# Row scores 48 slots ahead, key tiles loaded earlier and in pairs, weight stores one tile later, and output copies tied to TensorE, in an attention and MLP block on one core

## The chip, the core and the metric

The kernel runs on one core of one Trainium2 chip. The metric is the device time of one launch in microseconds (us). A core has five engines that run their own instruction streams in order: PE (TensorE, matrix multiply), DVE (VectorE), ACT (ScalarE), POOL (GpSimd) and SP (SyncE, which here does nothing but issue DMAs). They meet only through semaphores. An instruction that waits holds back all that stands behind it on its engine.

## The reference

One transformer block for 2048 rows of width 576, with 32 heads of 18 and an MLP of width 4608, all in f32:

```python
mod = (silu(c) @ w_mod).reshape(1, 6, 1, 576)
sa, ca, ga, sb, cb, gb = mod[:, 0], ..., mod[:, 5]
h = layernorm(x) * (1 + ca) + sa
q, k, v = heads(h @ wqkv)                      # 32 heads of 18
p = softmax(q @ k.T * 18 ** -0.5)
x = x + ga * ((p @ v) @ wo)
h = layernorm(x) * (1 + cb) + sb
x = x + gb * (silu(h @ w1) @ w2)               # 576 -> 4608 -> 576
```

## The kernel before

**Tiling.** The queries are cut into four blocks of 512 rows (b = 0 to 3), the heads into eight quads of four. A quad of one block is 32 *slots*. In slot s two score products stand on PE, in two half-slots j = 0 and 1:

- `psa` (`slot_mm`): 128 queries against 512 keys of one head, rows of scores. DVE takes their maximum into `mx` (L692). When a quad's 32 slots are through, `max_a` and `max_rows` turn the maxima, write them to DRAM (`mscr<-mt`, L717) and read them back as two extra rows of the query tile (`qt<-mscr`, L721).
- `psb` (`slot_b`): 128 keys against 512 queries, the transposed scores with the maxima already taken off by those two rows. ACT takes the exponential into a tile `pt` (L741).

`psa` runs `LEAD` slots ahead of `psb`, since a quad's `psb` needs the maxima of all its `psa`. The two of one half-slot use opposite halves of the array's rows and run side by side. The values products `psv` (L776, four heads of one 128-key tile at a time) read `pt` and use the whole array; `PB` tiles `pt` are in turn use.

**Key tiles.** `ka0..3` feed `psa`, `kb0..3` feed `psb`. A *chunk* is 512 keys of a quad: two tiles, one for each pair of heads (`hp`). `load_k` issues a chunk's four DMAs in one go, 8 slots before the chunk's first use, at the slot in which the tiles' last use has just been issued.

**Fillers.** Between the score and values products PE gets other work, from a list (`Filler`). For b = 0 it is the rest of the q and k projections (`psqk`), whose weights are loaded by DMAs that ACT issues (`qk_load`, L529). Then, while block b + 1 is in attention, it is block b's output projection, second layernorm and MLP (`post`). Block 3's MLP runs alone at the end. Products are made in f32 accuracy from a high and a low part of each operand. In the first pass over the MLP weights (`first`, beside block 1's attention) `weights` loads each piece raw into one of three buffers, POOL splits it (L836 to L838), and the split tile is stored to DRAM (`w1s`, `w2s`, `wos`, L839); later passes read the split tiles back (L829). The adds into the residual `x` are partly ACT copies `gt` (L899) followed by POOL adds (L900).

**What sets the order.** PE's order is written out by a planner in the kernel: `Plan` keeps a clock of PE and of the queues of ACT ("A") and DVE ("V"), with a fixed cost per operation (`TMAX` for a row maximum, `TEXP` for an exponential), and the loop at the end takes values products, a filler piece or a half-slot, whichever its rules allow. The start (layernorm 1, v and first q, k projections, the first `LEAD` slots' `psa`) is ordered by a small list scheduler (`Start`). On ACT, DVE, POOL and SP the framework orders the instructions by its own estimate of when each is ready.

Of the kernel before, what the change touches and what calls it, by code (L numbers as in the profile page):

```python
# [18 lines left out]
P = 128  # L19
# [6 lines left out]
KT = 5  # L26
# [13 lines left out]
LEAD = 40  # L40
# [3 lines left out]
NKA, NKB = 4, 4  # L44
KLD = 8
# [16 lines left out]
PB = 10  # L62
# [12 lines left out]
TMAX, TEXP = 690, 600  # L75
# [24 lines left out]
class Plan:  # L100
# [22 lines left out]
    def advance(self):  # L123
        while True:
            best = None
            for e, q in self.queue.items():
                if q:
                    s = max(self.free[e], q[0][0])
                    if s <= self.t and (best is None or s < best[0]):
                        best = s, e  # L130
            if best is None:
                return
            s, e = best
            _, _, dur, done = heapq.heappop(self.queue[e])
            self.free[e] = s + dur
            if done is not None:
                done(s + dur)
# [203 lines left out]
def tile_adaln_block(ctx: ExitStack, tc: tile.TileContext, x, wqkv, wo, w1, w2, c, wfirst, wcol, out):  # L341
# [14 lines left out]
    kas = [at1.tile([P, 512], F32R, name=f"ka{i}") for i in range(NKA)]  # L356
    kbs = [at1.tile([P, 512], F32R, name=f"kb{i}") for i in range(NKB)]
# [99 lines left out]

    class Pair:
# [137 lines left out]
    state = {"now": 0, "p": 0, "ka": 0, "kb": 0, "b": 0, "tail": False, "tail2": False}  # L596
# [3 lines left out]
    def add_qk(steps):  # L600
        def load(i):
            which, m, _ = steps[i]
            fill.add(0, lambda: qk_w.update({i: qk_load(which, m, i)}))

        for i, (which, m, pairs) in enumerate(steps):
            for n in sum(pairs, ()):
                names = [("qkx"[which], m, n)]
                for p in range(len(GQ)):
                    fill.add(MMC * len(GQ[p]), lambda i=i, which=which, m=m, n=n, p=p: qk_one(which, m, n, qk_w[i], p), name=names, need=bank_need if p == 0 else None, mode="full")
                    if n == pairs[0][0] and p == 0 and i + 1 < len(steps):  # L610
                        load(i + 1)
                    if i >= MI and p == len(GQ) - 1 and mods:
# [3 lines left out]
                        fill.add(200, lambda a=mt_: mod_piece(*a), mode="full")  # L616

# [37 lines left out]
    def load_k(ring, n):  # L655
        i, kc = divmod(n, NKEY)
        qd = i % NQUAD
        tiles = kas if ring == "a" else kbs
        for hp in range(2):
            kt_ = tiles[state["k" + ring] % len(tiles)]  # L660
            state["k" + ring] += 1
            h = 4 * qd + 2 * hp
            for j in range(2):
                nc.sync.dma_start(f(kt_[64 * j:64 * j + 54, :]),
                                  f(kscr[(h + j) * DH:(h + j + 1) * DH, :, kc * 512:(kc + 1) * 512].rearrange("d c s -> (d c) s")))
            quads.setdefault(i, {})[ring, kc, hp] = kt_
# [10 lines left out]
    def slot_load(s):  # L677
        i = s // 32
        if s % 32 == (22 if i == 0 else 14) and i + 1 < NQ:
# [43 lines left out]
    def slot_b(s, j):  # L723
# [3 lines left out]
        if j == 0:  # L727
            if s % 8 == 0 and s and s + 8 < 32 * NQ:
                load_k("b", s // 8 + 1)
# [5 lines left out]
            t["P"][kt, hp] = pts[s % PB]  # L735
# [3 lines left out]
        mm(ps, lhsT=t["b", kt // 4, hp][64 * e:64 * e + 56, kt % 4 * P:(kt % 4 + 1) * P],  # L739
# [86 lines left out]
    def weights(w, src, scr, first, gate=None):  # L826

        if not first:
            nc.sync.dma_start(f(w), f(scr))  # L829
            return  # L830
        n = w.shape[2] // 2
        for cs in (slice(0, n), slice(n, 2 * n)):
            raw = mp["p"].tile([P, 320], F32, tag="raw", name="raw", bufs=3)[:, :n]
            nc.sync.dma_start(raw, src[:, cs])
            if gate is not None:
                nc.gpsimd.tensor_tensor(raw, raw, gate[:, cs], op=ALU.mult)  # L836
            nc.gpsimd.tensor_copy(w[:, 1, cs], raw)
            nc.gpsimd.tensor_tensor(w[:, 0, cs], raw, f(w[:, 1, cs]), op=ALU.subtract)  # L838
        nc.sync.dma_start(f(scr), f(w))  # L839

# [15 lines left out]
    def post(b):  # L856
# [7 lines left out]
        def o_T(kt):  # L864
# [7 lines left out]
            nc.scalar.activation(hi[:n], src[:n], AF.Copy)  # L872
# [179 lines left out]
        def add_mlp1(i, w2n=()):  # L1052

            for part in range(NG):
# [34 lines left out]
    def start_tasks(st):  # L1089
# [285 lines left out]
        for n in range(2 * NKB):  # L1375
            ones_t.append(dma(40e3, lambda n=n: nc.sync.dma_start(f(kbs[n // 2][64 * (n % 2) + 54:64 * (n % 2) + 56, :]), f(oscr[:, :512])), [t], 8.4))
        q_in = [dma(443e3, lambda: load_quad(0), stored[QM, 0, 0], 5.5)]
        for kc in range(4):
            k_in[0, kc] = dma(443e3, lambda kc=kc: load_k("b" if kc < 2 else "a", kc), stored[KM, 0, kc] + ([k_in[0, kc - 1]] if kc else []), 5.5 + kc)
# [3 lines left out]
        for s in range(LEAD):  # L1383
            i, w = divmod(s, 32)
            if s in (24, 32):
                kc = s // 8 - 3
                k_in[1, kc] = dma(443e3, lambda kc=kc: load_k("a", 4 + kc), stored[KM, 0, kc] + stored[KM, 1, kc] + [mm_t, k_in[(0, 3) if kc == 0 else (1, 0)]], 10 if kc else 8.8)
# [77 lines left out]
    while now < 2 * (total + LEAD) or pend or later:  # L1465
        plan.advance()
        if not mp and fill.pos == len(fill.items):
# [7 lines left out]
        room = state["p"] + (now % 2 == 0) <= PB  # L1475
# [7 lines left out]
        elif not mp:  # L1483
# [98 lines left out]
```

## Time and profile before

| | us |
|---|---|
| median of 3 runs | 2464.89 |
| lowest and highest | 2458.97, 2471.31 |
| profiled execution | 2463.14 |
| its span | 2461.4 |
| PE busy in the span | 2359.8 |
| DVE busy | 1789.9 |
| ACT busy | 1497.0 |
| POOL busy | 628.6 |

How to read it: the span goes from the first to the last instruction of the profiled execution, whose own time is 1.7 us longer. "Busy" is the union of an engine's instructions. The ends of PE's matmuls are modelled, so a short wait can hide inside a busy PE. Times in rows are counted from the span's start. In a row of the timeline the bracket holds the idle time of the engine just before the row and what ended it; "x4" is a row of four instructions. The stages by time: start to 168, attention of block 0 with the q and k fillers to 537, the change to the MLP pools and the first output projection to 600, block 1 with the first pass over the weights to about 1143, block 2 to 1668, block 3 to 2172, then block 3's MLP alone.

### The profile page before, as it was taken

What the parts mean: (1) busy time and instruction counts of PE and PEld (TensorE: products, weight loads), DVE (VectorE), ACT (ScalarE), POOL (GpSimd) and SP (SyncE); (2) the same over time, 40 slices, a digit from 0 to 9 for tenths busy, and PEclk for the clock granted to TensorE, in tenths of its full rate; (3) what the DMA queues carried; (4) which work ended last, traced back from release to release, by engine and by line L of the source; (5) the groups of instructions that cost most, each with busy time, mean ns of one, the idle gap of its engine ahead of it and who ended that gap; (6) DMA issues with size and microseconds to landing.
All of it is one profiled execution on the core that took longest, in us unless ns stands there. A gap on an engine that the chain in (4) does not pass through costs nothing.

```text
span 2461.4 us, 52349 instructions
## 1 busy us (share of the span) xinstructions
PE 2359.8 (96%) x19952; PEld 1585.1 (64%) x19952; DVE 1789.9 (73%) x3110; ACT 1497.0 (61%) x2736; POOL 628.6 (26%) x763
## 2 busy tenths in 40 slices
PE   6989999998999999999999999998999999989999
PEld 4864444433556666766667667775666766678998
DVE  7868888876777888777888888887888788234333
ACT  4227777765566777666677677775677677732121
POOL 5201111122565666554211111112211111110000
PEclk9999999999899999999999999999999999999999
DMA  7744445454466676664545554453655454426563
GB/s 242 250 154 151 147 150 161 143 160 146 144 202 195 227 227 209 206 211 164 182 147 202 171 178 157 164 179 117 217 176 162 155 197 165 133 90 241 183 214 119
DMA packets 201458, 433.01 MB, mean 176 GB/s; under 512 B 31354, under 2 KB 67610, under 8 KB 201210
## 3 DMA queue, kind: packets, MB, share of 16 engines
q1 hardware_dynamic: 196618, 427.37, 52.4%
q8 instruction: 160, 2.62, 0.5%
q10 hardware_dynamic: 4592, 2.29, 0.4%
q14 instruction: 88, 0.72, 0.1%
HBM read 338.53 MB, written 86.33 MB: 173 GB/s over the span
## 4 chain that ended last, share of the span: by engine, by line
PE 82%; DMA 6%; DVE 5%; POOL 2%; ACT 2%; issue 2%; SPq 1%; ACTq 0%; POOLq 0%; DVEq 0%
PE ps L480 25%; PE psv L776 17%; PE psa L690 12%; PE ps L474 10%; PE psb L739 8%; PE psqk L561 4%; DVE mx L692 2%; PE psv L480 2%; PE psp L480 1%; DMA raw<-in_w 1%; DMA mscr<-mt 1%; PE psv L1238 1%; PE psqk L1238 1%; PE psqk L480 1%; PE psp L474 1%
## 5 line engine op out<-in xcount | busy, mean ns | idle before, releaser
L692 DVE TENSOR_REDUCE mx<-psa 128x1 f32<-128x512 f32 x2048 | 1333.0, 684 | 334.5 <-PE psb L739 199.6
L741 ACT ACTIVATE pt<-psb 128x512 f32<-128x512 f32 x2048 | 1150.5, 598 | 511.0 <-PE psb L739 350.0
L739 PE MATMUL psb<-qt,kb 56*128 56x512 f32 x2048 | 772.6, 427 | 39.2 <-ACT pt L741 22.0
L690 PE MATMUL psa<-ka,qt 54*128 54x512 f32 x2016 | 739.4, 420 | 10.9 <-DVE mx L692 8.7
L690 PEld LDWEIGHTS psa<-ka,qt 54*128 54x128 f32 x2016 | 344.1, 188 | 316.3 <-DVE mx L692 213.4
L776 PE MATMUL psv<-pt,vt 128*32 128x512 f32 x4096 | 521.4, 608 | 2.0 <-ACT ov L780 2.0
L480 PE MATMUL ps<-w2t,g 64*128 64x288 f32 x4992 | 418.4, 296 | 0.2
L739 PEld LDWEIGHTS psb<-qt,kb 56*128 56x128 f32 x2048 | 357.4, 187 | 90.3 <-ACT pt L741 61.0
L480 PEld LDWEIGHTS ps<-w2t,g 64*128 64x128 f32 x4992 | 390.7, 188 | 32.7 <-DVE mx L692 13.4
L480 PE MATMUL ps<-hh,w1t 64*128 64x512 f32 x2160 | 384.7, 395 | 1.7 <-DVE x L896 1.6
L480 PEld LDWEIGHTS ps<-hh,w1t 64*128 64x128 f32 x2160 | 216.4, 186 | 60.6 <-DVE mx L692 10.9
L1016 POOL TENSOR_TENSOR g<-etmp,g 128x512 fp32r<-128x512 f32 x108 | 138.8, 1305 | 397.6 <-ACT g L1015 318.0
L776 PEld LDWEIGHTS psv<-pt,vt 128*32 128x32 f32 x4096 | 98.5, 109 | 211.7 <-issue 203.4
L900 POOL TENSOR_TENSOR x<-x,gt 128x288 f32<-128x288 f32 x116 | 92.7, 801 | 427.0 <-ACT gt L899 426.9
L480 PE MATMUL ps<-hl,w1t 64*128 64x512 f32 x864 | 181.1, 392 | 0.0
L896 DVE TENSOR_TENSOR x<-ps,x 128x288 f32<-128x288 f32 x184 | 83.8, 456 | 122.0 <-PE ps L474 76.6
L474 PE MATMUL ps<-w2t,g 128*128 128x288 f32 x960 | 132.9, 299 | 7.4 <-ACT g L1015 5.9
L474 PEld LDWEIGHTS ps<-w2t,g 128*128 128x128 f32 x960 | 130.6, 191 | 9.9 <-ACT g L1015 6.3
L1012 ACT ACTIVATE eq<-ps 128x512 f32<-128x512 f32 x36 | 21.5, 598 | 146.4 <-PE ps L474 146.4
L474 PE MATMUL ps<-hh,w1t 128*128 128x512 f32 x360 | 106.9, 390 | 0.5 <-DVE hh L415 0.5
L480 PEld LDWEIGHTS ps<-hl,w1t 64*128 64x128 f32 x864 | 90.5, 187 | 16.5
L1013 DVE SCALAR_TENSOR_TENSOR etmp<-etmp 128x512 f32<-128x512 f32 x108 | 78.1, 759 | 22.1 <-ACT etmp L1012 21.3
(141 smaller groups left out, 2025.4 us busy)
## 6 DMA issues: line engine op xcount, KB each, us to landing
w1t<-w1s SPq DMA_DIRECT2D x108, 640.0 KB
w2t<-w2s SPq DMA_DIRECT2D x108, 576.0 KB
kb<-kscr SPq DMA_DIRECT2D x512, 108.0 KB
ka<-kscr SPq DMA_DIRECT2D x504, 108.0 KB
w1s<-w1t SPq DMA_DIRECT2D x36, 640.0 KB
w2s<-w2t SPq DMA_DIRECT2D x36, 576.0 KB
vt<-vscr SPq DMA_DIRECT2D x32, 608.0 KB
qt<-qscr SPq DMA_DIRECT2D x128, 108.0 KB
```

The costliest lines, as they stand in the source:

```text
L474: mm(self.ps[late], lhsT=lhsT, rhs=rhs, start=(i == 0), stop=(i == self.n - 1))
L480: done = mm(self.ps[g], lhsT=lhsT[rows], rhs=rhs[rows], start=(s == 0), stop=(s == 2 * self.n - 1))
L561: mm(qk_ps[0], lhsT=w[b][:, kt, :], rhs=(hTl if a else hTh)[:, kt, n * 512:(n + 1) * 512], start=(i == 0), stop=(i == 13))
L690: mm(ps, lhsT=t["q"][64 * j:64 * j + 54, hp, stt * P:(stt + 1) * P], rhs=t["a" if ("a", kc, hp) in t else "b", kc, hp][64 * j:64 * j + 54, ...
L692: return lambda: nc.vector.tensor_reduce(t["mx"][:, 2 * j + hp, stt, kc:kc + 1], ps, axis=AX.X, op=ALU.max)
L739: mm(ps, lhsT=t["b", kt // 4, hp][64 * e:64 * e + 56, kt % 4 * P:(kt % 4 + 1) * P], rhs=t["q"][64 * e:64 * e + 56, hp, :], start=True, sto ...
L741: nc.scalar.activation(t["P"][kt, hp][:, e, :], ps, AF.Exp, scale=SCALE)
L776: mm(t["ps"][32 * h:32 * h + 32, :], lhsT=t["v"][:, c0:c0 + 32], rhs=t["P"][kt, h // 2][:, h % 2, :], start=(kt == 0), stop=(kt == NKT - 1 ...
L896: nc.vector.tensor_add(c["x1"][j][:, hs], ps, c["x1"][j][:, hs])
L900: nc.gpsimd.tensor_add(c["x1"][j][:, hs], c["x1"][j][:, hs], t)
L1013: nc.vector.scalar_tensor_tensor(t, t, 1.0, u, op0=ALU.add, op1=ALU.mult)
L1016: (nc.vector if last else nc.gpsimd).tensor_tensor(g[:, 1, :], t, f(g[:, 0, :]), op=ALU.subtract)
```

## The change

- `LEAD` 40 to 48: the start holds eight more slots of `psa`.
- The key tiles of `psb` go from 4 to 6, and `pt` from 10 to 9 tiles. `load_k` now loads one tile (a pair of DMAs) at a time, one to five slots after its buffer's last use: `ka` tiles 11 slots ahead of their first use, `kb` tiles 14 and 13.
- The planner's costs: a row maximum takes DVE for 605 instead of 690 ns and its result comes 85 ns later (`TLAT`); an exponential takes ACT for 495 instead of 600 ns and its result comes 100 ns later.
- `weights` puts a split tile's store at the next call of `weights`, ahead of that tile's loads. The two `w1` tiles of a step are loaded at parts 0 and 2 instead of both at part 0.
- The weights of the q and k fillers are loaded from SP's queue instead of ACT's, and split some parts later than they are loaded.
- `after_pe` makes the ACT copies `th<-ou` of the output projection wait for the last `psb` issued before them.

```diff
-LEAD = 40
+LEAD = 48
-PB = 10
+PB = 9
-TMAX, TEXP = 690, 600
+TMAX, TEXP = 605, 495
+TLAT = {"A": 100, "V": 85}
...
             self.free[e] = s + dur
             if done is not None:
-                done(s + dur)
+                done(s + dur + TLAT[e])
...
-    kbs = [at1.tile([P, 512], F32R, name=f"kb{i}") for i in range(NKB)]
+    kbs = [at1.tile([P, 512], F32R, name=f"kb{i}") for i in range(6)]
...
+    def after_pe(ins):
+        if state["pe"] is not None:
+            tc.add_manual_dep(ins.ins, state["pe"].ins.name, SYNC, reason="its turn by the plan")
...
-        raw = qk_raw.pop(i)() if i in qk_raw else raw_load(qk_src(which, m), KT * P, nc.scalar)
+        if i not in qk_raw:
+            raw = raw_load(qk_src(which, m), KT * P, nc.sync)
+            qk_raw[i] = lambda: raw
+
+    def qk_split(i):
+        raw = qk_raw.pop(i)()
         hi = hi_part(raw)
         return hi, lo_part(raw, hi)
...
+    def weights(w, src, scr, first, gate=None):
+        while stores:
+            w_, scr_ = stores.pop()
+            nc.sync.dma_start(f(scr_), f(w_))
...
-        nc.sync.dma_start(f(scr), f(w))
+        stores.append((w, scr))
...
-        if (s + KLD) % 8 == 0 and 32 <= s + KLD < 32 * NQ:
-            load_k("a", (s + KLD) // 8)
+        n, w = divmod(s, 8)
+        if w == 1:
+            if s == LEAD + 1:
+                load_k("a", n + 1, 0)
+            load_k("a", n + 1, 1)
+        elif w == 5:
+            load_k("a", n + 2, 0)
...
-            if s % 8 == 0 and s and s + 8 < 32 * NQ:
-                load_k("b", s // 8 + 1)
+            if s % 8 in (2, 4):
+                load_k("b", s // 8 + 2, s % 8 // 2 - 1)
...
-            nc.scalar.activation(hi[:n], src[:n], AF.Copy)
+            after_pe(nc.scalar.activation(hi[:n], src[:n], AF.Copy))
...
-                if part == 0 and i + 2 < NFT:
-                    fl.add(0, lambda: w_load(i + 2))
-                    fl.add(0, lambda: w_load(i + 3))
+                if part in (0, 2) and i + 2 < NFT:
+                    fl.add(0, lambda n=i + 2 + part // 2: w_load(n))
...
-            if s in (24, 32):
+            if s in (24, 32, 40):
...
-        room = state["p"] + (now % 2 == 0) <= PB
+        room = state["p"] + (now % 2 == 0) <= len(pts)
```

Three places show how the order of instructions moves. The first is PE at the end of the start: the last v projections (`psv<-wv`), then `psa` alone, then the first `psb`. Before:

```order
L480 MATMUL psv<-wv,hTh 128x288 x4
L690 MATMUL psa<-ka_81,qt 128x512 x6
L690 MATMUL psa<-ka_82,qt 128x512
L739 MATMUL psb<-qt,kb_84 128x512
L690 MATMUL psa<-ka_82,qt 128x512
```

Now:

```order
L483 MATMUL psv<-wv,hTh 128x288 x4
L726 MATMUL psa<-ka_81,qt 128x512 x6
L726 MATMUL psa<-ka_82,qt 128x512 x8
L726 MATMUL psa<-ka_83,qt 128x512 x8
L726 MATMUL psa<-ka_80,qt 128x512
L776 MATMUL psb<-qt,kb_84 128x512
```

The eight added slots stand in one run behind the v projections: 22 `psa` in a row ahead of the first half-slot, where there were 6.

The second is ACT at the change from block 1 to block 2, from the copy `ov` of block 1's last values to the last two copies `th<-ou`, which read what the DMAs from `ov` bring. Before:

```order
L780 ACTIVATE ov<-psv_14312 128x512
L741 ACTIVATE pt_2095<-psb 128x512 x2
L1015 ACTIVATE g<-etmp 128x512 x2
L741 ACTIVATE pt_2096<-psb 128x512 x2
L741 ACTIVATE pt_2097<-psb 128x512 x2
L872 ACTIVATE th<-ou 128x512
L741 ACTIVATE pt_2098<-psb 128x512 x2
L741 ACTIVATE pt_2089<-psb 128x512 x2
L872 ACTIVATE th<-ou 64x512
```

Now:

```order
L817 ACTIVATE ov<-psv_14460 128x512
L1037 ACTIVATE g<-etmp 128x512
L778 ACTIVATE pt_2150<-psb 128x512
L1037 ACTIVATE g<-etmp 128x512
L778 ACTIVATE pt_2150<-psb 128x512
L894 ACTIVATE th<-ou 128x512 x3
L778 ACTIVATE pt_2151<-psb 128x512 x2
L778 ACTIVATE pt_2152<-psb 128x512 x2
L778 ACTIVATE pt_2153<-psb 128x512 x2
L778 ACTIVATE pt_2154<-psb 128x512 x2
L778 ACTIVATE pt_2155<-psb 128x512 x2
L894 ACTIVATE th<-ou 128x512
```

Twelve exponentials now stand between `ov` and the fourth copy, where six stood.

The third is SP in block 1, at the thirteenth store of a split `w1` tile, among the raw loads that POOL splits and the key loads. Before:

```order
L834 DMA raw<-in_w 128x320
L664 DMA ka_80<-kscr 54x512 x2
L834 DMA raw<-in_w 128x320
L839 DMA w1s<-w1t 128x1280
L834 DMA raw<-in_w 128x288 x2
L664 DMA kb_86<-kscr 54x512 x2
L664 DMA ka_81<-kscr 54x512
L664 DMA kb_87<-kscr 54x512
L839 DMA w1s<-w1t 128x1280
```

Now, at the same place of the weights:

```order
L644 DMA raw<-in_w 128x320
L695 DMA ka_82<-kscr 54x512 x2
L695 DMA kb_88<-kscr 54x512 x2
L644 DMA raw<-in_w 128x320
L637 DMA w1s<-w1t 128x1280
L695 DMA ka_83<-kscr 54x512
L695 DMA kb_89<-kscr 54x512
L644 DMA raw<-in_w 128x288 x2
```

The stores stand between the same raw loads as before; what moved is the key loads, which here fill tiles that are used later, and which stand among the stores.

More of the change, by code (lines that the diff above doesn't have):

```diff
@@ L616, in add_qk @@
                         fill.add(200, lambda a=mt_: mod_piece(*a), mode="full")
+    stores = []
+    def weights(w, src, scr, first, gate=None):
+        while stores:
+            w_, scr_ = stores.pop()
+            nc.sync.dma_start(f(scr_), f(w_))
+        if not first:
+            nc.sync.dma_start(f(w), f(scr))
+            return
+        n = w.shape[2] // 2
+        for cs in (slice(0, n), slice(n, 2 * n)):
+            raw = mp["p"].tile([P, 320], F32, tag="raw", name="raw", bufs=3)[:, :n]
+            nc.sync.dma_start(raw, src[:, cs])
+            if gate is not None:
+                nc.gpsimd.tensor_tensor(raw, raw, gate[:, cs], op=ALU.mult)
+            nc.gpsimd.tensor_copy(w[:, 1, cs], raw)
+            nc.gpsimd.tensor_tensor(w[:, 0, cs], raw, f(w[:, 1, cs]), op=ALU.subtract)
+        stores.append((w, scr))
     steps = []
@@ L653, in load_quad, with load_k @@
         t["mx"] = at1.tile([P, 4, NST, NKEY], F32, tag="mx", name="mx", bufs=2)
-    def load_k(ring, n):
+    def load_k(ring, n, hp):
         i, kc = divmod(n, NKEY)
[L657 to L666, printed above, removed]
+        if i >= NQ:
+            return
+        kt_ = kas[n % 2 * 2 + hp] if ring == "a" else kbs[n % 3 * 2 + hp]
+        h = 4 * (i % NQUAD) + 2 * hp
+        for j in range(2):
+            nc.sync.dma_start(f(kt_[64 * j:64 * j + 54, :]),
+                              f(kscr[(h + j) * DH:(h + j + 1) * DH, :, kc * 512:(kc + 1) * 512].rearrange("d c s -> (d c) s")))
+        quads.setdefault(i, {})[ring, kc, hp] = kt_
     def load_v(i):
@@ L824, in tile_adaln_block @@
     left = []
[L826 to L839, printed above, removed]
     def prefetch(b):
@@ L1466, in tile_adaln_block @@
         plan.advance()
-        if not mp and fill.pos == len(fill.items):
+        if "p" not in mp and fill.pos == len(fill.items):
             open_mlp()
```

27 lines of the change are left out of this document (15 added, 12 removed).

## The prediction

> **What bounds the kernel now.** I read the page's busy lines and its chain first, then a table by stage, then what PE itself waited for, then the timeline at the longest waits.
>
> ```profile
> span 2461.4 us, 52349 instructions
> PE 82%; DMA 6%; DVE 5%; POOL 2%; ACT 2%; issue 2%; SPq 1%; ACTq 0%; POOLq 0%; DVEq 0%
> ```
>
> PE carries 82% of the chain that ends last. The stages (length, then PE busy, with the granted clock behind the engines) tell where the rest lies:
>
> ```profile
> 0.00:168.00 168.00, 136.03 (x1147) 115.83 (x1148) 126.96 (x272) 55.20 (x96) 45.53 (x55) 0.96 0.68 220
> 168.00:537.00 369.00, 367.56 (x2198) 154.80 (x2197) 310.13 (x527) 276.31 (x533) 40.93 (x31) 1.00 0.47 150
> 537.00:600.00 63.00, 48.57 (x238) 18.26 (x238) 40.04 (x68) 35.28 (x66) 24.52 (x35) 0.85 0.59 188
> 600.00:1143.00 543.00, 521.40 (x4824) 354.12 (x4820) 421.15 (x702) 358.45 (x650) 321.91 (x446) 0.97 0.60 196
> 1143.00:1668.00 525.00, 516.40 (x5040) 355.16 (x5040) 424.30 (x720) 367.26 (x667) 93.49 (x94) 0.99 0.52 173
> 1668.00:2172.00 504.00, 496.25 (x4832) 338.74 (x4836) 354.65 (x610) 350.13 (x639) 90.19 (x90) 0.99 0.48 158
> ```
>
> Block 0's attention (168 to 537) leaves PE 1.4 us idle at full clock: there only less work helps. From 537 to 2172 PE is idle for 14.4 + 21.6 + 8.6 + 7.8 = 52 us, most of it beside block 1, and each longer wait is followed by half clock. What PE waited for, all in all (total, times, longest):
>
> ```profile
> PE psb L739 <- ACT pt L741: 22.0, 26, 4.8
> PE psb L739 <- DMA qt<-mscr: 9.7, 4, 3.4
> PE psa L690 <- DVE mx L692: 8.7, 15, 2.8
> PE psv L480 <- ACTq L491: 6.2, 1, 6.2
> PE psb L739 <- DMA ka<-kscr: 5.0, 1, 5.0
> PE psb L739 <- DMA kb<-kscr: 1.9, 3, 0.8
> ```
>
> Stretches behind such waits, with the granted clock behind the five engines:
>
> ```profile
> 127.00:135.00 8.00, 5.93 (x52) 5.80 (x54) 2.74 (x6) 1.31 (x3) 0.00 (x0) 0.57 0.75 249
> 545.00:554.00 9.00, 8.79 (x31) 3.31 (x32) 3.27 (x5) 4.41 (x9) 8.59 (x12) 0.50 0.76 245
> 592.00:602.00 10.00, 4.97 (x17) 1.95 (x17) 4.29 (x7) 3.77 (x8) 1.27 (x1) 0.66 0.35 107
> 789.40:793.00 3.60, 3.60 (x24) 3.48 (x26) 1.80 (x6) 2.01 (x4) 0.00 (x0) 0.53 0.77 209
> 1150.00:1158.00 8.00, 5.09 (x26) 2.87 (x27) 3.33 (x6) 3.79 (x7) 1.27 (x1) 0.59 0.32 102
> ```
>
> Length times the missing share is what the half clock takes: 3.4, 4.5, 3.4, 1.7 and 3.3 us.
>
> **The change, part by part.**
>
> *Planner's costs.* Maxima and exponentials in a row:
>
> ```profile
> L692 DVE TENSOR_REDUCE mx<-psa 128x1 f32<-128x512 f32 x2048 | 1333.0, 684 | 334.5 <-PE psb L739 199.6 <-PE psa L690 120.6 <-PE ps L480 0.3
> 163.53 5.47 DVE L692 TENSOR_REDUCE mx<-psa 128x1 f32<-128x512 f32 x9 [0.94 <-PE psa L690]
> 1300.95 1.07 ACT L741 ACTIVATE pt<-psb 128x512 f32<-128x512 f32 x2
> ```
>
> One maximum shows 684 ns, but nine in a row end after 5.47 us, (5.47 - 0.68) / 8 = 0.60 each; two exponentials take 1.07 for one of 0.60, so 0.47 to 0.49. The new 605 and 495 are the true rates. They change nothing on DVE and ACT themselves; they let the planner put half-slots closer together, and PE changes less often between half-array and full-array work. What a change costs:
>
> ```profile
> 300.85 0.40 PE L561 MATMUL psqk<-hTh,wqh 128*128 128x512 f32 x1
> 301.18 0.50 PE L690 MATMUL psa<-ka,qt 54*128 54x512 f32 x1
> ...
> 301.52 0.62 PE L690 MATMUL psa<-ka,qt 54*128 54x512 f32 x2
> 301.75 0.39 PE L739 MATMUL psb<-qt,kb 56*128 56x512 f32 x1
> 302.07 1.07 PE L776 MATMUL psv<-pt,vt 128*32 128x512 f32 x8
> ```
>
> Starts within a mode are 0.23 apart (301.52 to 301.75); leaving full-array work costs 0.33 and 0.34 for two steps, entering it 0.32, so about 0.30 for a pair of changes. The order holds 908 changes before and 849 now: 59 / 2 x 0.30 = -9 us, nearly all on the path since PE bounds those stages.
>
> *Eight more slots in the start.* 16 maxima stand in one run with nothing left beside them: 16 x 0.60 = +9.6 us, +11 with a colder clock behind. They leave block stages that PE bounds, so nothing is given back there. Bounds: +2 (8 x 0.23, PE alone) to +15. What it buys: `psb` of a quad starts 17 instead of 9 slots after the last `psa` issue; a slot is about 525 / 256 = 2 us, so 16 us more for `mscr` and back. The waits on it were 1.8, 3.4, 1.5 and 3.0 us, far below 16.
>
> *Weight loads of the q and k fillers.* ACT's own queue held it in the start, and PE's turn (a nop of ACT, L491) stood behind:
>
> ```profile
> 128.40 0.56 ACTq L529 DMA_DIRECT2D raw<-in_wqkv  x1
> 129.22 0.60 ACT L572 ACTIVATE qkhl<-psqk 128x512 fp32r<-128x512 f32 x1 [6.46 <-DMA raw<-in_wqkv]
> ```
>
> On SP the loads hold no engine that computes. Bounds: -9.6 (6.2 and 3.4 of clock) to 0, if SP, which has the k stores and key loads of quad 1 behind the loads, now waits in ACT's stead. I take -8, since half of those loads are not needed until block 0. The Trainium skill, "DMA: Bandwidth & Descriptors", section "Issuing engines are not separate DMA queues", says that issuing from several engines saves only the sequencer's issue time. By that rule this term would be the 0.6 us of an issue, and the sum 7 us less; the row of 6.46 speaks against it here, since what ACT lost is a wait in its stream and not the issue.
>
> *Copies tied to PE, and the block changes.*
>
> ```profile
> 543.52 1.15 ACT L872 ACTIVATE th<-ou 128x512 fp32r<-128x512 f32 x2 [4.35 <-DMA qscr<-qkhl]
> 545.21 0.79 PE L739 MATMUL psb<-qt,kb 56*128 56x512 f32 x1 [4.78 <-ACT pt L741]
> 597.49 1.28 PE L739 MATMUL psb<-qt,kb 56*128 56x512 f32 x2 [5.03 <-DMA ka<-kscr]
> 1151.77 0.63 ACT L872 ACTIVATE th<-ou 128x512 fp32r<-128x512 f32 x1 [3.47 <-DMA ou<-ov]
> 1674.87 0.63 ACT L872 ACTIVATE th<-ou 128x512 fp32r<-128x512 f32 x1 [4.27 <-DMA ou<-ov]
> ```
>
> ACT stood in a copy whose input was late, the exponentials behind it, PE behind those. In block 0 the copies now stand some 40 exponentials behind the last projection (4 to 6 before), in blocks 1 and 2 twelve instead of six behind `ov`; at about 1 us each (two per slot) the landing, some 9 us after `ov`, is covered. Block 0: 4.8 and 4.5 of clock go. The wait of 5.0 at 597 was key loads queued on SP behind `ou<-ov`; loaded 11 to 14 slots instead of 8 ahead (6 to 12 us more) they are in time: 5.0 and 3.4, and 1.8 and 1.6 for the `mscr` wait at 583. Sum 21; I take -20. Blocks 1 and 2: 2.9 + 3.3 and, by the same pattern, 2.9 + 1.3 + 3.4; I take -12 of 14. What is late next is the projection behind the copies, which waits for all five.
>
> *Block 1.* Three `mscr` waits (7.8) with three half clocks (1.7 each) and three `kb` waits (1.9): -14. The longer ring of `kb`, bought with one `pt`, costs nothing where the planner finds room; values runs grow in the new order. The stores I cost at 0: among the raw loads they stand where they stood. What stays is ACT in `gt` behind POOL, which waits for raw loads:
>
> ```profile
> 788.44 0.41 ACT L899 ACTIVATE gt<-ps 128x288 f32<-128x288 f32 x1 [3.62 <-POOL x L900]
> 789.39 0.66 PE L739 MATMUL psb<-qt,kb 56*128 56x512 f32 x1 [1.71 <-ACT pt L741]
> ```
>
> Three such waits, and one of 2.8 at 637 with 17 us of half clock, hold about 19 us; raw loads spread over parts 0 and 2 may ease some: -5, bounds -19 to +5.
>
> *Clock.* The row of 1.71 at 789 is followed by 3.4 us at 0.53. The Trainium skill, "TensorE: Matmul & The Clock Gate", section "What's actually happening", lets the clock fall only after an idle window of about 3.4 us. By that rule only the waits of 6.2, 4.8, 5.0 and 3.4 would carry a clock term, and the sum would be some 10 us less; the trace disagrees with it at 1.71.
>
> *Sum.* -9 + 11 - 8 - 20 - 12 - 14 - 5 = -57. Waits that go are partly replaced by the next latest; I give back 7 and take -50: 2463.1 - 50 = 2413. The profiled execution stands 1.8 below the median of the runs shown, so this is a time for both.
>
> **Rivals.** *(a) Block 1 becomes like block 2.* It then loses all its waits: 543 - 525 = 18 more at 600 to 1143 instead of 14 + 5, and what I gave back and held back (7 + 1 + 2 + 2) goes too: about 2395. For it: same PE work in both stages. Against it: POOL's 322 us there against 93, with raw loads, splits and adds in one stream.
>
> *(b) SP stays the limit.*
>
> ```profile
> SPq L664 <- PE psa L690: 382.3, 241, 9.7
> SPq L664 <- PE psb L739: 262.9, 195, 8.1
> SPq L839 <- POOL w2t L838: 28.8, 21, 5.7
> ```
>
> SP stood 645 us in key loads that waited for PE, with everything queued behind. If it still does, `mscr` and keys are late again: block 1's 14, 7 of block 0's 20 and the 8 of the start are lost, leaving 2440. Against it: loads now issue after their buffer's last use, so the waits get shorter.
>
> *(c) Slower: the planner has no slack left.* At 605 it believes DVE free 85 ns sooner per maximum. Where other DVE work cuts in, the half-slot now waits on PE instead. At all 2048 maxima this is 2048 x 0.085 = +174; it undoes my sum from 57 / 174 = 33% of them, and at half of them gives 2500. Against it: 0.60 in a row, and PE's waits on maxima were 8.7 in all.
>
> **How the numbers follow.** My case (2395 to 2428) 0.58, (a) 0.14, (b) and mixtures of it up to 2450 0.16, no net change 0.06, (c) 0.06. A measurement of this kernel tells about 0.5% (12 us) from no change. Slower 0.06 by (c); same 0.07 with a tail of (b); faster 0.87. The range 2385 to 2445 takes in (a) and (b) and leaves out (c); it is no narrower since the start's +2 to +15 and block 1's -19 to +5 add to the spread.
>
> **What the changed profile would show.** Right: no row of PE waiting on `qt<-mscr`, `ka` or ACTq of over 1 us; `th<-ou` without a bracket of DMA; 537 to 600 at a clock above 0.95; a run of some 25 maxima at the end of the start, first `psb` about where it was; SP's wait on L664 (now `load_k` at another line) far below 645. Wrong: PE waits on `mx` well above 8.7 (c), or `mscr` and key rows still there (b).

## The result, and the profile after

| | before | after |
|---|---|---|
| median of 4 runs, us | 2466.80 | 2438.51 |
| lowest and highest | 2458.97, 2471.31 | 2432.60, 2447.21 |
| profiled execution | 2463.14 | 2447.21 |
| its span | 2461.4 | 2445.4 |

The ratio is 0.9891, with a 95% interval of 0.9851 to 0.9931: 1.1% faster, 28 us. I had forecast 2413, about 50 us faster. The sign was right and the size about twice too large. The two profiled executions lie 16 us apart, the medians 28, because the profiled one after is the slowest of its four runs and the one before stands 3.7 below its median. A second set of six runs (below) gave 0.9909 (0.9887 to 0.9931), 23 us.

The page after, its first line and the chain by engine:

```profile
span 2445.4 us, 52248 instructions
PE 79%; DMA 6%; DVE 6%; POOL 3%; ACT 3%; issue 2%; SPq 1%; ACTq 0%; POOLq 0%; DVEq 0%
```

PE bounds as before (79% of that chain, 82% before). For the stages I cut both traces at the same places of the work: the first values product of quads 0, 8, 16 and 24 and the last one. The order of the columns is length, busy PE, PEld, DVE, ACT, POOL, granted clock, DMA share, GB/s. After:

```profile
0.00:173.90 173.90, 148.14 (x1178) 120.96 (x1178) 138.67 (x292) 56.94 (x99) 45.50 (x55) 0.93 0.70 226
173.90:579.50 405.60, 396.68 (x2396) 167.64 (x2394) 340.30 (x581) 303.05 (x586) 56.09 (x54) 1.00 0.48 152
579.50:1134.80 555.30, 523.11 (x4849) 365.95 (x4852) 428.85 (x712) 358.27 (x659) 332.66 (x454) 0.97 0.62 199
1134.80:1655.70 520.90, 514.35 (x5041) 366.72 (x5042) 420.25 (x719) 363.04 (x667) 92.77 (x93) 1.00 0.52 173
1655.70:2156.20 500.50, 496.70 (x4818) 346.12 (x4820) 342.94 (x595) 347.36 (x641) 92.17 (x92) 1.00 0.47 159
```

Before, the stage of block 1 by the same cut:

```profile
590.00:1143.30 553.30, 526.13 (x4849) 355.72 (x4848) 426.93 (x713) 362.61 (x659) 323.49 (x447) 0.96 0.60 195
```

By stages (us), with the experiments that the argument rests on:

| | start | block 0 | block 1 | block 2 | block 3 | rest |
|---|---|---|---|---|---|---|
| before | 173.7 | 416.3 | 553.3 | 524.9 | 504.1 | 289.1 |
| after | 173.9 | 405.6 | 555.3 | 520.9 | 500.5 | 289.2 |
| after, second profile | 172.3 | 405.5 | 552.7 | 519.6 | 500.6 | 289.2 |
| before + tie | 171.0 | 408.4 | 539.0 | 518.9 | 497.3 | 289.4 |
| before + tie + LEAD 48 | 179.7 | 411.6 | 541.5 | 523.1 | 497.0 | 289.6 |
| after, old costs | 176.1 | 411.8 | 547.1 | 519.3 | 497.0 | 289.5 |
| after, LEAD 40 | 164.3 | 403.8 | 544.1 | 519.2 | 501.0 | 289.2 |

Block 0 gained 11 us and blocks 2 and 3 together 8. Block 1, from which I took 19 us and part of the first block change, is as long as before. Most of the miss against the forecast lies there. What PE waited for after (total, times, longest):

```profile
PE psb L776 <- ACT pt L778: 27.4, 25, 7.2
PE psa L726 <- DVE mx L728: 7.6, 18, 0.9
PE ps L483 <- ACT gt L921: 5.0, 2, 2.9
PE psqk L569 <- ACT qt L573: 4.3, 3, 1.6
```

The waits on `mscr`, on `ka` and `kb` and on ACT's queue in the start are gone, as forecast: 9.7 + 5.0 + 1.9 + 6.2 us. The last row above is new and stands in the q and k fillers of block 0. And PE's wait on exponentials stands at 27.4 where it was 22.0. The next view tells why: what ACT waited for within block 1. Before (590 to 1143) and then after (580 to 1135):

```profile
ACT gt L899 <- POOL x L900: 9.7, 3, 3.6
ACT th L872 <- DMA ou<-ov: 5.7, 1, 5.7
```

```profile
ACT gt L921 <- POOL x L922: 22.3, 6, 6.2
ACT etmp L1034 <- POOL g L1038: 8.6, 7, 2.8
ACT th L894 <- DMA ou<-ov: 6.6, 2, 6.4
```

ACT's waits behind POOL went from 9.7 to 30.9 us. One of them, in the timeline after: POOL waits for a raw load, its add into `x` stands behind that piece, the next copy `gt` needs the buffer that the add reads, the exponentials stand behind the copy, and PE behind these:

```profile
713.37 1.55 POOL L646 TENSOR_TENSOR raw<-raw,gb 128x288 f32<-128x288 f32 x2 [1.92 <-DMA raw<-in_w]
714.87 0.80 POOL L922 TENSOR_TENSOR x<-x,gt 128x288 f32<-128x288 f32 x1
715.70 0.41 ACT L921 ACTIVATE gt<-ps 128x288 f32<-128x288 f32 x1 [4.63 <-POOL x L922]
716.65 1.28 PE L776 MATMUL psb<-qt,kb 56*128 56x512 f32 x2 [2.73 <-ACT pt L778]
```

So block 1 shows two kinds of wait. One kind I had taken for a lack of lead (`mscr`, keys), and the change removes it. The other is POOL's stream of raw loads and splits, which runs at its own pace: POOL's work there is the same (323 and 333 us busy), and when PE comes sooner, ACT finds POOL less far in its work.

### The profile page after: what moved, and what is told of

It is laid out like the page before. It is cut to its first block, busy times and chain, and to the rows that moved or that the text cites. A ratio compares the mean times of both kernels' runs of the same rounds, so it can differ in the third digit from the quotient of the medians.

```text
span 2445.4 us, 52248 instructions
## 1 busy us (share of the span) xinstructions
PE 2352.7 (96%) x19952; PEld 1616.0 (66%) x19952; DVE 1783.8 (73%) x3110; ACT 1483.1 (61%) x2736; POOL 631.2 (26%) x763
## 4 chain that ended last, share of the span: by engine, by line
PE 79%; DMA 6%; DVE 6%; POOL 3%; ACT 3%; issue 2%; SPq 1%; ACTq 0%; POOLq 0%; DVEq 0%
PE ps L483 23%; PE psv L813 16%; PE psa L726 12%; PE ps L477 10%; PE psb L776 8%; PE psqk L569 4%; DMA raw<-in_w 3%; DVE mx L728 2%; PE psp L483 2%; PE psv L483 2%; DMA ka<-kscr 1%; PE psqk L483 1%; ACT pt L778 1%; PE psqk L1259 1%; PE psv L1259 1%
## 5 line engine op out<-in xcount | busy, mean ns | idle before, releaser
L728 DVE TENSOR_REDUCE mx<-psa 128x1 f32<-128x512 f32 x2048 | 1318.8, 684 | 311.7 <-PE psb L776 188.6
L778 ACT ACTIVATE pt<-psb 128x512 f32<-128x512 f32 x2048 | 1131.8, 599 | 487.7 <-PE psb L776 325.4
L776 PE MATMUL psb<-qt,kb 56*128 56x512 f32 x2048 | 756.3, 428 | 28.7 <-ACT pt L778 27.4
L726 PE MATMUL psa<-ka,qt 54*128 54x512 f32 x2016 | 702.7, 420 | 9.4 <-DVE mx L728 7.6
L726 PEld LDWEIGHTS psa<-ka,qt 54*128 54x128 f32 x2016 | 337.9, 187 | 302.6 <-DVE mx L728 213.1
L813 PE MATMUL psv<-pt,vt 128*32 128x512 f32 x4096 | 512.8, 603 | 1.0 <-ACT ov L817 0.9
L483 PE MATMUL ps<-hh,w1t 64*128 64x512 f32 x2160 | 395.7, 394 | 3.0 <-DVE x L918 1.5
L483 PEld LDWEIGHTS ps<-hh,w1t 64*128 64x128 f32 x2160 | 243.2, 185 | 41.4 <-DVE mx L728 9.2
L483 PE MATMUL ps<-hl,w1t 64*128 64x512 f32 x864 | 197.7, 392 | 0.0
L483 PEld LDWEIGHTS ps<-hl,w1t 64*128 64x128 f32 x864 | 105.3, 186 | 9.8
```

Source lines behind the costliest of these rows:

```text
L483: done = mm(self.ps[g], lhsT=lhsT[rows], rhs=rhs[rows], start=(s == 0), stop=(s == 2 * self.n - 1))
L726: mm(ps, lhsT=t["q"][64 * j:64 * j + 54, hp, stt * P:(stt + 1) * P], rhs=t["a" if ("a", kc, hp) in t else "b", kc, hp][64 * j:64 * j + 54, ...
L728: return lambda: nc.vector.tensor_reduce(t["mx"][:, 2 * j + hp, stt, kc:kc + 1], ps, axis=AX.X, op=ALU.max)
L776: state["pe"] = mm(ps, lhsT=t["b", kt // 4, hp][64 * e:64 * e + 56, kt % 4 * P:(kt % 4 + 1) * P], rhs=t["q"][64 * e:64 * e + 56, hp, :], s ...
L778: nc.scalar.activation(t["P"][kt, hp][:, e, :], ps, AF.Exp, scale=SCALE)
L813: mm(t["ps"][32 * h:32 * h + 32, :], lhsT=t["v"][:, c0:c0 + 32], rhs=t["P"][kt, h // 2][:, h % 2, :], start=(kt == 0), stop=(kt == NKT - 1 ...
```

## The experiments

All ratios are to the kernel before, run beside each on the same chip, with the 95% interval; its median in these sets was 2464.5 to 2465.8.

**The changed kernel again.**

> The changed kernel once more, with more rounds, to have its ratio to the kernel before to a few tenths of a per cent, and a second profile. The first profiled execution was 16 us shorter than that of before, the medians lay 28 us apart. Expected: median 2436 to 2442; in the profile block 1's long waits (ACT in the copy gt behind POOL's add into x, 4.4 to 6.2 us each; ACT in tanh behind POOL's g) at the same places, since the order is the same. If those waits are chance, they stand elsewhere or are shorter.

2441.97, ratio 0.9909 (0.9887 to 0.9931). Most of the waits behind POOL stand at the same places, between 684 and 1054, with other lengths (ACT in `gt` 19.8, in tanh 7.4); a few came or went. So they are not chance, but their size varies. I use 2442 below.

**The planner's costs alone, and the change without them.**

```diff
 # on the kernel before
-TMAX, TEXP = 690, 600
+TMAX, TEXP = 605, 495
...
-                done(s + dur)
+                done(s + dur + TLAT[e])
```

> The kernel before with the planner's new costs alone (605, 495 and the later results). My prediction's term: fewer mode changes, -9 us, so about 2456 against 2465. Rival (the planner has no slack left): PE waits more on maxima and exponentials, in block 1 above all, and the time stays or rises: 2465 to 2480.

2451.12, ratio 0.9948 (0.9929 to 0.9967): -14, a little more than the -9 of my sum, but not where the sum had it. Cut like the table above, the stages took 169.1, 407.7, 547.3, 524.4, 510.5 and 289.7: less in the start, in block 0 and in block 1, nothing in block 2, and 6 us more in block 3. In block 0 the wait of 4.8 at the block change went (all of PE's waits behind exponentials there are 3.4 us, 7.2 before), which my sum had given to the tie.

```diff
 # on the changed kernel
-TMAX, TEXP = 605, 495
-TLAT = {"A": 100, "V": 85}
+TMAX, TEXP = 690, 600
+TLAT = {"A": 0, "V": 0}
```

> The changed kernel with the planner's costs of before (690, 600, no delay of results), all else as changed. If the new costs bring what I gave them: +9, about 2448. If they are what made block 1 lose (half-slots so close that a late ACT is felt at once), it is faster than the changed kernel: 2425 to 2432, and block 1 takes back some of its 6 us.

2438.62, ratio 0.9886 (0.9865 to 0.9907): with the old costs the changed kernel is as fast, if anything 3 us faster. By stages the new costs bring 6 in block 0 and 2 to 4 in the start, and lose 6 to 8 in block 1 and 4 in block 3. The first -14 is therefore not a price that the costs keep in any surroundings. A wait of the size that they lose in block 1 stands at the first block change. With the old costs the DMAs `ou<-ov` leave as soon as `ov` is complete (both 592.1), ACT waits 1.1 us in the copies behind them and PE 1.7. With the new ones they leave 5.6 us after `ov` (582.7 to 588.3; 5.4 in the second profile), ACT waits 6.6 and PE 7.2. This divides all runs: 3.3 to 6.9 us in every kernel with the new costs, at most 0.4 in every kernel with the old ones. Why blocks 2 and 3 do not get shorter, though the order changes less often there between half-array and full-array work, I did not settle: the last six quads of block 2, where PE is idle for 2 to 3 us in either kernel, took 381.7 us before (1286.5 to 1668.2) and 383.6 with the costs alone (1264.9 to 1648.5).

**The tie of the copies, taken out and alone.**

```diff
 # on the changed kernel
-            after_pe(nc.scalar.activation(hi[:n], src[:n], AF.Copy))
+            nc.scalar.activation(hi[:n], src[:n], AF.Copy)
```

> The changed kernel without the tie of the copies th<-ou to the last psb. They stand up to 35 instructions earlier on ACT; PE's order is the same. By my sum most of the -20 and -12 hang on it: 8 to 15 us slower, about 2452, with ACT in th<-ou behind DMA rows of 3 to 6 us and PE waits behind them at the block changes. Rival (the key loads ahead of their time and SP's order did it, and at the first change ou<-ov is late in either order): within 4 us.

2472.09, ratio 1.0036 (1.0021 to 1.0051): without the tie the change is slower than the kernel before. The tie is worth 30 us in it. ACT's longest wait in a copy was 10.5 us instead of 6.4:

```profile
594.03 0.63 ACT L894 ACTIVATE th<-ou 128x512 fp32r<-128x512 f32 x1 [10.47 <-DMA ou<-ov]
```

```diff
 # on the kernel before
+    def after_pe(ins):
+        if state["pe"] is not None:
+            tc.add_manual_dep(ins.ins, state["pe"].ins.name, SYNC, reason="its turn by the plan")
...
-        mm(ps, lhsT=t["b", kt // 4, hp]...
+        state["pe"] = mm(ps, lhsT=t["b", kt // 4, hp]...
...
-            nc.scalar.activation(hi[:n], src[:n], AF.Copy)
+            after_pe(nc.scalar.activation(hi[:n], src[:n], AF.Copy))
```

> The kernel before with the tie of the copies th<-ou to the last psb alone. Taken out of the changed kernel the tie was worth 30 us. If it is worth that by itself too, 2435; by my sum's parts (4.8 and 4.5 at the first change, 12 at the later ones) 2444. Rival: without the earlier key loads and with SP's order of before, the waits on mscr and on key tiles take its place: 2455 or more.

2431.72, ratio 0.9873 (0.9855 to 0.9890): -34 by itself, more than the whole change. Blocks 0 and 1 are 22 us shorter, blocks 2 and 3 13, and my two terms were 20 and 12. The wait of 5.0 at 597 is gone too, though the key tiles are loaded no sooner than before: so what I had put down to the key loads was the copy again, in which ACT stood until 596.3 (the row of 5.7 above). The `mscr` waits are still there (three of the four, 12.2 us, in block 1), and POOL holds ACT little. What PE waited for between 570 and 1115, what ACT waited for there, and the stage:

```profile
PE psb L743 <- DMA qt<-mscr: 14.4, 4, 4.6
PE psb L743 <- ACT pt L745: 4.9, 6, 2.5
```

```profile
ACT gt L903 <- POOL x L904: 5.4, 4, 3.0
```

```profile
579.40:1118.40 539.00, 515.72 (x4849) 349.60 (x4848) 426.71 (x712) 362.06 (x658) 322.57 (x447) 0.98 0.62 200
```

**The eight slots.**

```diff
 # on the changed kernel
-LEAD = 48
+LEAD = 40
```

> The changed kernel with LEAD back at 40, all else as changed. By my sum the eight slots cost 11 in the start and buy the waits on the maxima's way through DRAM (about 16 with their half clocks): about 5 us slower than the changed kernel, 2447, with PE waits on qt<-mscr back in blocks 0 and 1. Rival: the start's run of maxima costs more than 11 because it also drops the clock (6.8 us of half clock stand there in the changed kernel), and block 1 is held by the weight stream anyway, so the waits bought were not worth it: 3 to 8 us faster, 2434 to 2439.

2423.37, ratio 0.9834 (0.9817 to 0.9850): the rival's side, and beyond its range. The eight slots cost 19 us: about 8 to 10 in the start, near my term, and 9 to 11 in block 1 by the two profiles of the changed kernel, where I had booked a gain.

```diff
 # on the kernel before with the tie
-LEAD = 40
+LEAD = 48
...
-        if s % 32 == (22 if i == 0 else 14) and i + 1 < NQ:
+        if s % 32 == (26 if i == 1 else 14) and i + 1 < NQ:
...
-            if s in (24, 32):
+            if s in (24, 32, 40):
...
-                k_in[1, kc] = dma(443e3, ..., k_in[(0, 3) if kc == 0 else (1, 0)]], 10 if kc else 8.8)
+                k_in[1, kc] = dma(443e3, ..., k_in[(0, 3) if kc == 0 else (1, kc - 1)]], 10 if kc == 2 else 8.8)
```

> The kernel before with the tie and LEAD 48 (and the third chunk of ka in the start that this needs). My sum for the eight slots: +11 in the start, -16 for the mscr waits (14.4 with the tie alone, and their half clocks): about 2427. By the run of the changed kernel with LEAD 40, where the eight slots cost 19: the mscr waits go but ACT's waits behind POOL come in their place, 2441 or more.

2444.37, ratio 0.9912 (0.9896 to 0.9929): +13 on the tie alone. This pair shows the exchange at its cleanest. The `mscr` waits of 14.4 us are gone to the last row, and yet block 1 went from 539.0 to 541.5. ACT now waits for POOL 23.7 us in `gt` instead of 5.4, and PE 13.2 for ACT instead of 4.9, so PE's idle time in block 1 fell by 2 us alone (23.3 to 21.3); its busy time rose by 4.5 (515.7 to 520.2), which I did not settle:

```profile
ACT gt L903 <- POOL x L904: 23.7, 7, 4.7
```

```profile
PE psb L743 <- ACT pt L745: 13.2, 14, 2.4
```

```profile
591.30:1132.80 541.50, 520.23 (x4845) 356.27 (x4844) 430.23 (x712) 362.55 (x659) 328.47 (x447) 0.99 0.61 199
```

**POOL's part of block 1 taken away, in three ways.** Each is on the changed kernel. First the adds:

```diff
-            if hf == 0 or state["tail"]:
+            if hf == 0 or b == 0 or state["tail"]:
                 nc.vector.tensor_add(c["x1"][j][:, hs], ps, c["x1"][j][:, hs])
...
-                    plan.op("AV"[g == 0], plan.t + 200, 440, c["pp"].release[g])
+                    plan.op("AV"[g == 0 or b == 0], plan.t + 200, 440, c["pp"].release[g])
...
-                plan.op("AV"[hf == 0], plan.t + 200, 440, c["p2"].release[hf])
+                plan.op("AV"[hf == 0 or b == 0], plan.t + 200, 440, c["p2"].release[hf])
```

> The changed kernel with the second half of each add into x done by DVE from PSUM during block 1 (as the first half is), instead of an ACT copy and a POOL add; DVE gets some 50 x 0.46 = 23 us more there. Theory (POOL's stream of raw loads and splits is what block 1 waits for now, through the copy gt): the PE waits of 2.7, 2.1, 2.9 and 4.3 us and their half clocks go, -12 to -15, about 2425. Rival (SP's late raw loads hold PE in another way, or DVE becomes the limit of block 1): within 4 us of the changed kernel, with waits on maxima in their place.

2439.92, ratio 0.9899 (0.9881 to 0.9917): inconclusive by time, 2 us below the changed kernel. The waits in `gt` went, but those of tanh behind POOL's `g` grew from 8.6 to 14.2 us. Then `g` as well:

```diff
-                (nc.vector if last else nc.gpsimd).tensor_tensor(g[:, 1, :], t, f(g[:, 0, :]), op=ALU.subtract)
+                (nc.vector if last or b == 0 else nc.gpsimd).tensor_tensor(g[:, 1, :], t, f(g[:, 0, :]), op=ALU.subtract)
...
-                    chain([..., ("A", 630)], plan.t + 200, ...)
+                    chain([..., ("A", 630)] + [("V", 690)] * (b == 0), plan.t + 200, ...)
```

> As the kernel with the x adds on DVE, and the subtraction of g's high part in block 1 on DVE too instead of POOL (36 of them, 0.7 us each). Theory (POOL's stream behind the raw loads holds ACT): the remaining PE waits behind ACT's tanh of 2.1 to 2.5 us go, 4 to 8 us faster than with the x adds alone, in blocks 0 and 1 together about 944. Rival (DVE becomes block 1's limit): PE waits on maxima, no faster.

2424.99, ratio 0.9841 (0.9827 to 0.9855): -17, now that ACT waits for POOL neither in `gt` nor behind `g`. Block 1 takes 531.8 us, and DVE, 462 us busy there, does not become its limit (PE's waits on maxima are 4.0 us). Third, POOL keeps its work and gets its loads sooner:

```diff
-            raw = mp["p"].tile([P, 320], F32, tag="raw", name="raw", bufs=3)[:, :n]
+            raw = mp["p"].tile([P, 320], F32, tag="raw", name="raw", bufs=4)[:, :n]
...
-        rec = att.tile([P, 16], F32, name="rec", bufs=2)
+        rec = att.tile([P, 16], F32, name="rec", bufs=1)
```

> The changed kernel with four raw weight buffers instead of three (and one buffer less of a small tile, rec). PE's order is the same. If POOL is late because a raw load can only start when a buffer is free (POOL waits 89 and 55 us for raw loads in block 1), the copies gt wait less, and block 1 loses 5 to 12 us: 2430 to 2437. Rival (raw loads are late because SP stands in other waits ahead of them): within 3 us.

2429.93, ratio 0.9860 (0.9846 to 0.9874): -12. With the same order on PE, POOL waited less for raw loads and ACT less in `gt` (block 1 of this kernel):

```profile
POOL raw L646 <- DMA raw<-in_w: 66.3, 35, 6.1
POOL w1t L647 <- DMA raw<-in_w: 39.4, 17, 5.9
```

```profile
ACT gt L921 <- POOL x L922: 6.7, 2, 6.4
```

```profile
579.70:1116.50 536.80, 515.45 (x4845) 362.34 (x4844) 427.06 (x712) 358.32 (x659) 330.00 (x451) 0.98 0.62 205
```

In the changed kernel these three waits were 88.9, 54.7 and 22.3. So a good part of POOL's lateness is that a load starts only when a buffer is free; a wait of 6.4 us in `gt` and some 106 us of POOL's own waits on raw loads are left.

**The stores, and the queue of ou<-ov.** Both on the changed kernel:

```diff
-        stores.append((w, scr))
+        nc.sync.dma_start(f(scr), f(w))
```

> The changed kernel with each split tile stored at once, as before, instead of at the next call. I had costed the later store at 0. If SP stands less in waits for POOL's split ahead of raw loads thanks to the later store, this one is slower: POOL waits more than 88 and 57 us on raw loads in block 1, and 3 to 8 us are lost. If the cost is 0: within 3 us, 2439 to 2445.

2441.30, ratio 0.9910 (0.9893 to 0.9927): the later store changes nothing, as my 0 had it.

```diff
-                nc.sync.dma_start(ou[r0:r0 + d1 - d0, kt, :], ov[32 * h + d0:32 * h + d1, :])
+                (nc.scalar if (b, qd) == (0, NQUAD - 1) else nc.sync).dma_start(ou[r0:r0 + d1 - d0, kt, :], ov[32 * h + d0:32 * h + d1, :])
```

> The changed kernel with the five DMAs ou<-ov of block 0's last quad issued by ACT instead of SP. In the changed kernel ov stood ready at 582.7, SP issued them from 588.3 on behind stores, raw loads and key loads, and ACT waited 6.4 us in th<-ou, PE 7.2. If SP's queue is what makes them late, the wait shrinks to under 3 us, less the 3.6 us that ACT spends issuing: 3 to 6 us faster, 2437. If the landing itself takes that long, no change.

2452.62, ratio 0.9953 (0.9939 to 0.9968): 11 us slower than the changed kernel. Issued by ACT, the DMAs went out at 588.9, no sooner than from SP (588.3), with the exponentials behind them:

```profile
588.88 4.33 ACTq L841 DMA_DIRECT2D ou<-ov  x5
593.26 1.08 ACT L778 ACTIVATE pt<-psb 128x512 f32<-128x512 f32 x2 [8.95 <-DMA ou<-ov]
```

`ov` was complete at 584.7, so something other than SP's queue held them here. The trace names the semaphores that they waited for. Each DMA of this program takes the next of eight semaphores in turn, and waits until the DMA that had it before has landed. The first `ou<-ov` waits for DVE, which made `ov`, and for the semaphore of a key load, `ka<-kscr`, that SP had issued at 584.75; the latter came at 588.8. None of the five waits for POOL, though POOL's subtraction `tl<-ou` (586.4 to 590.1) reads the same tile at the time. So the run does not test SP's queue: it put another wait, that for the semaphore, into ACT's stream. In the changed kernel `ov` was complete at 582.7, and SP issued nine other DMAs until 588.1. What makes them late in the changed kernel is thus the order that came with the new costs; with the old costs they leave at once, as shown above.

**Together.**

```diff
 # the changed kernel
-LEAD = 48
+LEAD = 40
 # and the edits of the adds, of g and of the four raw buffers, as above
```

> The changed kernel with LEAD 40, four raw buffers, and block 1's x adds and g's low parts on DVE. Alone they brought 19, 12 and 17 us against the changed kernel. If each took away a cause of its own (the start for LEAD, POOL's lateness for the other two), about 9 for the start stays beside some 17 to 20 in block 1: 2412 to 2416. If LEAD 40 brings waits on mscr back that the others laid bare, 2420 or more.

2415.68, ratio 0.9801 (0.9786 to 0.9817), as forecast for three causes that add up; PE's waits on `mscr` did not come back.

> The changed kernel with four raw buffers and block 1's x adds and g's low parts on DVE, LEAD at 48. Against the same with LEAD 40 (2416) this prices LEAD 48 when POOL's lateness is out of the way. If LEAD 48 costs its start alone: +8 to +10, about 2425, blocks 0 and 1 as long as with LEAD 40. If its 9 us in blocks 0 and 1 had another cause than POOL's lateness: +15 to +20, about 2433.

The same with LEAD 48 (only the edits of the adds, of `g` and of the buffers): 2421.80, ratio 0.9821 (0.9801 to 0.9841). With POOL out of the way the eight slots cost 6 us, in place of 19: by the profiles 162.8 to 175.7 in the start (which varies by some 5 us between profiles of the same work), and 530.9 to 529.5 in block 1. So what LEAD 48 lost in block 1 goes when POOL's part goes: it was lost to POOL.

> The kernel before with the tie of the copies, four raw buffers, and block 1's x adds and g's low parts on DVE; LEAD 40, the old costs, key loads and stores. If the tie and POOL's relief are two causes: 2432 less 10 to 15, about 2419, with the mscr waits (14 us) left. If the relief only lays bare those waits: 2427 or more.

The kernel before with the tie and the same three edits: 2411.02, ratio 0.9781 (0.9761 to 0.9802), the fastest of all, 31 us below the changed kernel. Block 1 is as short as block 2 (522.0), and its `mscr` waits nearly went without any more lead, so most of them was no lack of lead either; why they went I did not settle. POOL waits for raw loads as long as ever there, 96.0 and 41.0 us: that costs nothing once ACT does not wait for POOL. Against the changed kernel with LEAD 40 and the same edits, block 1 is 10.7 us shorter (520.2, 530.9 there): that one has a wait of PE of 7.9 us behind the copy at the first block change, this one has none. PE's waits in block 1, and the stage:

```profile
PE psa L694 <- DVE mx L696: 3.4, 8, 0.8
PE psb L743 <- issue: 3.0, 1, 3.0
PE psb L743 <- ACT pt L745: 1.5, 5, 0.3
PE psb L743 <- DMA qt<-mscr: 1.0, 1, 1.0
```

```profile
580.10:1100.30 520.20, 513.48 (x4846) 346.68 (x4844) 458.37 (x782) 351.73 (x622) 265.27 (x377) 0.99 0.63 207
```

## Why the prediction was right in sign and too large

*The block changes (-20 and -12).* The size is right for the tie alone, -34. The parts are not: the 5.0 and 3.4 that I gave to the earlier key loads came with the tie too, and the `mscr` wait at the first change stayed without LEAD 48. Inside the change less than half of the -20 came. PE's waits there of 4.8, 1.8 and 5.0 us became one of 7.2, behind a wait of 6.4 us in a copy, which came with the new costs and which my sum did not have:

```profile
593.54 0.63 ACT L894 ACTIVATE th<-ou 128x512 fp32r<-128x512 f32 x1 [6.44 <-DMA ou<-ov]
595.53 1.27 PE L776 MATMUL psb<-qt,kb 56*128 56x512 f32 x2 [7.16 <-ACT pt L778]
```

The clock of the change stands at 0.92 where I had asked for 0.95 and before showed 0.85:

```profile
537.00:600.00 63.00, 52.65 (x300) 20.77 (x300) 45.76 (x77) 40.92 (x76) 25.69 (x35) 0.92 0.65 211
```

I had called the landing some 9 us after `ov` and covered. It came 11 after `ov`'s last step, since the DMAs left 6 us late. The rows of the later changes (2.9 us of PE at each) are gone; blocks 2 and 3 gained 8 and not 13 because the new costs lost some 4 there.

*Eight more slots in the start (+11).* Right. The run of maxima is the forecast one, 16 longer than the nine of before, and (15.04 - 5.47) / 16 is 0.60 each:

```profile
153.87 15.04 DVE L728 TENSOR_REDUCE mx<-psa 128x1 f32<-128x512 f32 x25 [0.92 <-PE psa L726]
```

Measured in the start: +8.7 on the tie alone (171.0 to 179.7). Between the kernels with the loads on SP it is +10.7: 174.3 in the mean of ten profiles with LEAD 48, 163.6 in the mean of two with LEAD 40.

*What the slots buy (in block 1's -14, with 1.8 and 1.6 at the first change).* This is the step that failed most; the first block change, above, is the other. The waits on `mscr` went as forecast, but I counted each removed wait as time gained. It was gained only until the next engine that was behind: POOL, whose rows I had read and quoted (a raw load, the add, 3.62 us of ACT, 1.71 of PE) and costed as a small remainder of -5 with +5 as its worst end. Against the tie alone (539.0) block 1 is 14 to 16 us longer in the changed kernel, not 14 shorter: 541.5 with LEAD 48, 547.1 with the key loads, stores and other loads as well, 552.7 and 555.3 with the new costs. The first two steps go with ACT's waits behind POOL in `gt`, 5.4, 23.7 and 29.8 us; the last one brings the wait of 7.2 behind the copy at the first block change. My allowance for replaced waits, 7 us in all, was a guess where the rows of POOL's waits on raw loads in block 1, beside its 323 us of work, should have warned me that POOL comes next (the trace before):

```profile
POOL raw L836 <- DMA raw<-in_w: 80.0, 52, 11.9
POOL w1t L837 <- DMA raw<-in_w: 45.6, 28, 3.9
```

Rival (a), block 1 like block 2, is reached only once POOL is relieved, with the tie and LEAD 40: 520.2 us. Its forecast of 2395 does not follow from its own terms either: 18 in place of 14 + 5, and 12 given back, make 2402.

*Weight loads of the q and k fillers (-8).* The wait of 6.2 us on ACT's queue is gone. The start took 171.8 to 177.1 us, 174.3 in the mean, in ten profiles of kernels that have LEAD 48 and these loads on SP, and 179.7 in the one that has LEAD 48 and leaves them to ACT, so about -5; with LEAD 40 it is 163.6 in the mean of two against 171.0 in the mean of four (before, 173.7; costs alone, 169.1; tie alone, 171.0; the fastest kernel, 170.3), so about -7. The rule that I weighed there (the Trainium skill, "DMA: Bandwidth & Descriptors", section "Issuing engines are not separate DMA queues") would have given 0.6; the runs are nearer to the row than to the rule, as a wait in an engine's stream is not an issue.

*Planner's costs (-9).* -14 on the kernel before and +3 inside the change. That -14 is near -9 is luck. I had counted fewer changes between half- and full-array work at 0.30 a pair, on the path where PE bounds; blocks 2 and 3, where it does, took 6 us more with the costs alone. What they saved in block 0 was the wait at the block change, and inside the change the tie had already taken that. Rival (c), more waits on maxima, did not happen: 7.6 us after, 8.7 before.

*Rival (b), SP.* Its key loads waited as long as before, which I had forecast otherwise:

```profile
SPq L695 <- PE psb L776: 362.0, 212, 9.9
SPq L695 <- PE psa L726: 265.4, 197, 10.8
```

That is 627 against 645 us, and yet no `mscr` or key row is left. A long wait of a queue proves nothing by itself; what stood behind it in time for its use cost nothing.

*The sum by runs.* Taken in this order, before 2465; with the tie -34; with LEAD 48 on it +13; with the key loads, stores and weight loads -6 (2438.6, the change with the old costs); with the new costs +3: 2442. The key loads, the ring of six `kb` and the `w1` loads at parts 0 and 2 were not tried by themselves.

## What to carry to other kernels

A wait that is removed is worth its length only up to the next engine that is late at that place; look there for the engine with the longest own chain (here POOL: load, split, add) and ask what its lateness leaves of the gain, and look first for the cheap relief of that engine (one more buffer: 12 us). Buy lead only where its price, paid on every launch, is smaller than a wait that nothing else takes up. Of a bundle of edits, test each by itself on the kernel before: here one of them, the tie, brought more than all of them together.

## What the runs showed of the hardware

Half clock again followed a gap of under 3 us. In the changed kernel a gap of 2.88 us before 893.03 was followed by 3.40 us at 0.50:

```profile
893.03 0.53 PE L483 MATMUL ps<-w2t,g 64*128 64x288 f32 x4 [2.88 <-ACT gt L921]
893.80:897.20 3.40, 3.40 (x28) 3.40 (x27) 2.52 (x5) 1.42 (x4) 2.31 (x3) 0.50 0.49 135
```

The length of the gap alone does not decide: in the same trace a gap of 2.93 us before 813.37 left the clock at 1.00 (from 812 to 816). By the rule of the Trainium skill, "TensorE: Matmul & The Clock Gate", section "What's actually happening", an idle window of about 3.4 us is what lowers the clock; the gap of 2.88 does not agree with it.

The start also lost clock where the profile counts PE as busy but its 29 products came at DVE's pace, beside the 25 maxima:

```profile
156.00:170.00 14.00, 13.90 (x29) 6.65 (x28) 12.91 (x22) 1.75 (x3) 0.15 (x2) 0.52 0.51 161
```

That cost little there, as DVE set the pace: the 25 maxima stand back to back at 0.60 each.
